# Attention, soft mixture of experts and MLP in one kernel: the code behind the attention re-ordered by hand, the spread of G moved from engine copies to DMAs

## The chip, the core and the metric

The kernel runs on one core of a Trainium2 chip. The metric is device time in microseconds for one execution. A core has TensorE (PE in the rows; PEld is its weight load), VectorE (DVE), ScalarE (ACT), GpSimd (POOL) and SyncE (SP), which here only issues DMAs, from one queue, in order. Each engine executes its own instructions strictly in the order of the program and waits for semaphores of the others.

## The reference

```
q, k: (4, 8, 576, 64), rotated by position; attn = softmax(q k^T / 8) v
x = attn as (2304, 512)
logits = x @ phi                            # (2304, 32): 8 experts x 4 slots
d = softmax of logits over the 2304 tokens
s = d.T @ x                                 # slot inputs, (32, 512)
slot_out[e] = relu(s[e] @ w1[e]) @ w2[e]    # w1 (8,512,1024), w2 (8,1024,512)
c = softmax of logits over the 32 slots
y = c @ slot_out                            # (2304, 512), of rank 32
h = y @ w_in; g = h * sigmoid(h)            # w_in (512, 2048)
out = g @ w_out                             # w_out (2048, 512)
```

`w_in` and `w_out` come as 64-bit floats and are narrowed on the chip.

## The kernel before

**Attention** (until about 285 us of the trace) runs over 16 pairs of heads in an order written out by hand. It is not touched, except that its last piece, pair 15, is followed by the soft maximum over tokens of the last batch, done in two halves (`half(0)`, `half(1)`, L530 to L621).

**The tail.** `half(h)` does: logits (L545, L548, tile `lgh`), their maximum (L558), the exponentials (L567, ACT), their transposition (`dps`, L584, L586), the weighted sums `sps` (L595 with 128 tokens each, L599 with the 64 left over), and for half 1 `slots()` (L605): the two halves' sums are scaled and added by DVE (L608), turned by four products with a stacked identity (`si_ps`, L614) and copied to `si`, the slot inputs (L615). `x_15(1)` (L448 to L452) turns the last 64 + 256 tokens of the attention's output, which the last quarter of half 1's logits needs. `lt3_ps` (L945) turns the logits for the combine weights; DVE copies it (L947, L948).

**Experts** (L964 to L1106). `layer1` (L974) and `layer2` (L995) hold 32 slots as four groups of 32 columns of the array, one expert each, and stream the weights `w_0` to `w_63`, 512 KB a load; `more()` issues four further loads after each group, into slots that become free. 27 loads are issued during the attention (`W_LOADS`), the rest when its memory is released. `hidden_t` and `slot_t` turn the results by full-array transposes (L985, L1008). `combine` (L1017) computes the combine weights c on ACT and DVE, `combine_split` splits them into a high and a low part, `combine_t(b)` (tile `cst`, L1054, five transposes each for four blocks b, then DVE casts, L1061) lays them out as `cs`. From here on a scheduler of the framework orders the instructions, not the source, except where `tc.manual_schedule()` stands.

**Opening of the last stage** (L1226 to L1245, order by hand). G = slot_out @ `w_in` (32 x 2048) is made in pieces: the first 128 columns (`g0_ps`, L1229), 384 more (`g_product(0)`, L1192, and `g_spread`, L1213), then three times 512 (`g_product(1..3)`). G must lie in four groups of 32 partitions (high, high, low, low part: the tile `gs`). For pieces 1 to 3 `g_copy` (L1201) copies each of four quarters of a piece into the four groups: 16 copies of 32 x 128 a piece, 12 by ACT (L1206) and 4 by DVE (L1208).

**Last stage.** Three blocks of 768 tokens times 16 steps k. `hidden(j, k)` makes h for 128 columns of G in two halves: `hps` (L1152, PE, two PSUM buffers in all), sigmoid (L1156, ACT), product (L1159, DVE), the high part `ghi` (L1162, ACT), the low part `glo` (L1165, DVE), which frees the PSUM buffer. A step then has 18 products of 512 columns into six sums `ops` (L1257 to L1259: high*high, high*low, low*high). In block 0 `w_out` is also prepared: load (L126), `narrow` (L136 on ACT, L139 and L142 on DVE), split into `wo_hi` (L1134, ACT) and `wo_lo` (L1135, POOL); four of sixteen pieces are narrowed during the attention (`W_OUT_EARLY`). The last quarter of `w_in` is narrowed there too (`conv_last`).

Two "warm" products (L1221, `dummy`) without use stand in the opening; the scheduler placed one of them between the products of layer 2.

## Time and profile before

| | |
|---|---|
| median of 3 runs | 569.34 us (567.28 to 569.64) |
| the profiled execution | 568.04 us, of which its span is 566.2 us |
| PE busy | 542.6 us, 96% of the span |
| DVE, ACT, POOL busy | 317.5, 309.0, 111.6 us |
| share of PE in the chain that ended last | 77% (ACT 10%, DVE 7%, DMA 2%) |
| DMA | 88.53 MB, 156 GB/s on average |

Times in the rows are us from the start of the span. The profiled execution lies 1.30 us under the median, and 1.84 us of it lie outside the span. A busy PE means that matmuls are in flight, not that they follow each other without gaps.

### The profile page before, as it was taken

The page shows a single profiled execution, that of the slowest core. Times are in us where ns is not written, and L with a number is a line of the kernel's source. Part 1 is how long each engine was busy: PE and PEld are TensorE (multiplying, and loading weights), DVE is VectorE, ACT ScalarE, POOL GpSimd, SP SyncE. Part 2 cuts the span into 40 slices and gives each one's busy share as a digit, 9 for nine tenths or more (in the row PEclk, how much of TensorE's full clock was granted, in tenths as well). Part 3 has the DMA queues.
Part 4 walks back from the last instruction along what each step waited for, and adds up shares of the span by engine and source line. Part 5 has one row for each costly group of instructions (what it writes and reads, how often), then busy time and mean ns, then how long its engine had stood idle before and what let it go on. Part 6 is the DMA issues. An engine that isn't in the chain of part 4 may idle for free.

```text
span 566.2 us, 15233 instructions
## 1 busy us (share of the span) xinstructions
PE 542.6 (96%) x6281; PEld 438.1 (77%) x6281; DVE 317.5 (56%) x844; ACT 309.0 (55%) x613; POOL 111.6 (20%) x103
## 2 busy tenths in 40 slices
PE   8989999999999999999989979898999999999997
PEld 5667888889888898888853347686888888888885
DVE  4667666676665566653142356897464444644442
ACT  3657767666776576664422247987454334543332
POOL 3475333412333333100001030141000000000000
PEclk9999999999999999999999999999999999999999
DMA  8325777655663585653789965440020000300002
GB/s 328 114 83 203 236 245 250 201 180 174 219 226 125 201 284 192 230 171 116 294 309 375 389 280 186 148 125 25 1 111 1 0 1 1 113 0 1 0 2 111
DMA packets 36417, 88.53 MB, mean 156 GB/s; under 512 B 9830, under 2 KB 11644, under 8 KB 34428
## 3 DMA queue, kind: packets, MB, share of 16 engines
q1 hardware_dynamic: 36348, 87.57, 44.2%
q8 instruction: 49, 0.80, 0.6%
q14 instruction: 20, 0.16, 0.1%
HBM read 78.20 MB, written 7.60 MB: 152 GB/s over the span
## 4 chain that ended last, share of the span: by engine, by line
PE 77%; ACT 10%; DVE 7%; issue 3%; DMA 2%; POOL 0%; SPq 0%; ACTq 0%; DVEq 0%
PE u L420 10%; PE ops L1259 10%; PE ops L1257 10%; PE ops L1258 10%; PE st L387 8%; PE psmx L316 3%; PE hps L1152 3%; PE st_r L400 3%; ACT e L391 3%; PE xps L448 2%; PE l L974 2%; ACT relu L324 2%; PE u L414 2%; PE psmx L332 2%; PE warm_up L841 2%
## 5 line engine op out<-in xcount | busy, mean ns | idle before, releaser
L1159 DVE TENSOR_TENSOR hps<-hps,g 128x384 f32<-128x384 f32 x96 | 49.8, 561 | 84.6 <-ACT g L1156 84.3
L1156 ACT ACTIVATE g<-hps 128x384 f32<-128x384 f32 x96 | 42.3, 490 | 82.3 <-PE hps L1152 82.0
L1257 PE MATMUL ops<-wo_hi,ghi 128*128 128x512 f32 x216 | 84.7, 392 | 0.0
L337 DVE CUSTOM_DVE_ANT_0 relu<-psmx,relu 128x288 f32<-128x288 f32 x142 | 59.3, 454 | 45.0 <-ACT e L391 38.0
L1258 PE MATMUL ops<-wo_lo,ghi 128*128 128x512 f32 x216 | 84.4, 391 | 0.0
L1259 PE MATMUL ops<-wo_hi,glo 128*128 128x512 f32 x216 | 84.3, 390 | 0.0
L391 ACT ACTIVATE e<-st 128x512 f32<-128x512 f32 (+1 forms) x128 | 76.4, 650 | 10.4 <-PE st L387 10.4
L420 PE MATMUL u<-v,e 128*64 128x65 f32 x2048 | 80.1, 224 | 0.3 <-ACT e L391 0.3
L420 PEld LDWEIGHTS u<-v,e 128*64 128x64 f32 x2048 | 70.8, 137 | 6.7 <-issue 2.4
L324 ACT ACTIVATE relu<-psmx 128x576 f32<-128x576 f32 x63 | 40.9, 651 | 53.6 <-PE psmx L316 41.9
L266 POOL TENSOR_TENSOR raw<-raw,tab 128x576 f32<-128x576 f32 x28 | 40.3, 1438 | 114.4 <-DMA raw<-in_qk_dram 94.8
L1165 DVE TENSOR_TENSOR glo<-hps,ghi 128x384 fp32r<-128x384 f32 x96 | 49.4, 552 | 4.9 <-ACT ghi L1162 1.8
L1162 ACT ACTIVATE ghi<-hps 128x384 fp32r<-128x384 f32 x96 | 45.6, 492 | 10.1 <-DVE hps L1159 10.1
L1259 PEld LDWEIGHTS ops<-wo_hi,glo 128*128 128x128 f32 x216 | 40.6, 188 | 8.5
L1258 PEld LDWEIGHTS ops<-wo_lo,ghi 128*128 128x128 f32 x216 | 40.6, 188 | 7.5 <-issue 0.4
L1257 PEld LDWEIGHTS ops<-wo_hi,ghi 128*128 128x128 f32 x216 | 40.5, 188 | 7.4 <-issue 0.2
L263 POOL TENSOR_TENSOR raw<-raw,tab 128x576 f32<-128x576 f32 x28 | 41.3, 1475 | 0.0
L387 PE MATMUL st<-hi 64*128 64x256 f32 (+1 forms) x256 | 39.2, 300 | 0.0
L387 PE MATMUL st<-mq,neg_a 64*128 64x256 f32 (+1 forms) x256 | 38.2, 292 | 0.0
L387 PE MATMUL st<-hi,lo 64*128 64x256 f32 (+1 forms) x256 | 38.1, 292 | 0.0
L387 PE MATMUL st<-lo,hi 64*128 64x256 f32 (+1 forms) x256 | 38.1, 292 | 0.0
L431 DVE TENSOR_SCALAR r<-u 128x4 f32<-128x4 f32 (+1 forms) x32 | 5.2, 163 | 51.1 <-PE u L422 30.9
(233 smaller groups left out, 1008.4 us busy)
## 6 DMA issues: line engine op xcount, KB each, us to landing
w<-in_w_dram SPq DMA_DIRECT2D x64, 512.0 KB
...
```

The lines of the kernel that those rows point to most:

```text
L324: act.activation(out=r, in_=pair[:, :, 0:HS], func=ACTF.Relu)
L337: dve.tensor_tensor_reduce(out=r[:, hd], in0=t[hd], in1=r[:, hd], scale=1.0, scalar=-3.0e38, op0=ALU.add, op1=ALU.max, accum_out=mxs[p % 2 ...
L387: pe.matmul(st[:, hd, 0:n], lhsT=a, rhs=b, start=i == 0, stop=i == 3, skip_group_check=True)
L391: act.activation(out=e[:, :, 0:n], in_=st[:, :, 0:n], func=ACTF.Exp, scale=0.125)
L420: pe.matmul(u[q:q + 64, 2 * i + hd], lhsT=e[:, hd, o:o + 64], rhs=x[:, hd], start=n == 0 and i + hd == 0, stop=n == 4, skip_group_check=True)
L1156: act.activation(out=g[i], in_=t[i], func=ACTF.Sigmoid)
L1159: dve.tensor_tensor(out=t[i], in0=t[i], in1=g[i], op=ALU.mult)
L1162: act.activation(out=ghi[:, i], in_=t[i], func=ACTF.Copy)
L1165: dve.tensor_tensor(out=glo[:, i], in0=t[i], in1=ghi[:, i].bitcast(F32), op=ALU.subtract)
L1257: pe.matmul(t, lhsT=a, rhs=wo_hi[k], start=k == 0, stop=False)
L1258: pe.matmul(t, lhsT=a, rhs=wo_lo[k], start=False, stop=False)
L1259: pe.matmul(t, lhsT=b, rhs=wo_hi[k], start=False, stop=k == 15)
```

## The change

Behind the attention it does the following.

- Tail: `x_15(1)` goes ahead of two thirds of half 1's logits; the sums of half 1 are put in four column groups instead of two (`s_mm`); what lies in `s_b` is turned by a scaled identity `ss`, half 1's sums are copied by ACT and turned with 64 rows each, both into the same sum, and one copy gives `si`; the logits' transposes stand between; their copies go from DVE to ACT, and the sum of exponentials (`total`) behind `si`.
- Experts: the order of the source holds (`manual_schedule`); `combine` comes after `hidden_t(1)`; the blocks 2 and 3 of `combine_t` stand behind the last product of layer 2, ahead of and behind the turn of its result; the dummy products are gone. One more weight load (`w_27`) is issued during the attention, into the memory of the rotary table, and the slots of those behind it are given in the order in which the attention releases memory.
- Opening: `w_out` piece 0 is among the early ones (0, 3, 6, 10 instead of 3, 6, 9, 12), so that the opening narrows piece 1 alone; `ghi`'s first half goes ahead of the copy of `g_product(0)`; three products stand ahead of `g_spread`. `wo_lo` 0 and 1 go from DVE to POOL.
- Last stage: the second half of `hidden` in block 0 comes one sum later than the first; the 48 copies of `g_copy` become 48 DMAs from SP, a quarter of a piece per step; the loads of `w_out` take the next of three buffers in turn.

**The tail on PE**, from the product that adds up half 0's logits (`xps15_1` is `x_15(1)`, `dps3` the transposes of half 0). Before:

```order
L555 MATMUL lgh0_4879<-last_logits_4878,cst_sb_73 128x256
L548 MATMUL lgh1_4915<-xt12_4349,phi_sb_75 32x320 x4
L548 MATMUL lgh1_4915<-xt13_4621,phi_sb_75 32x320 x4
L548 MATMUL lgh1_4915<-xt14_4831,phi_sb_75 32x320 x4
L584 MATMUL dps3_4931<-cst_sb_73,last_logits_4878 128x32 x2
L448 MATMUL xps15_1_4935<-cst_sb_73,x15_4803 64x128 x4
L450 MATMUL xps15_1_4935<-cst_sb_73,x15_4803 64x64 x2
L548 MATMUL lgh1_4915<-xt15_4844,phi_sb_75 32x320 x4
```

And now:

```order
L566 MATMUL lgh0_4881<-last_logits_4880,cst_sb_76 128x256
L559 MATMUL lgh1_4917<-xt12_4351,phi_sb_78 32x320 x4
L459 MATMUL xps15_1_4922<-cst_sb_76,x15_4805 64x128 x4
L461 MATMUL xps15_1_4922<-cst_sb_76,x15_4805 64x64 x2
L559 MATMUL lgh1_4917<-xt13_4623,phi_sb_78 32x320 x4
L559 MATMUL lgh1_4917<-xt14_4833,phi_sb_78 32x320 x4
L559 MATMUL lgh1_4917<-xt15_4846,phi_sb_78 32x320 x4
L596 MATMUL dps3_4945<-cst_sb_76,last_logits_4880 128x32 x2
```

The turn of the last tokens has moved ahead of two groups of logits, the transposes of half 0 behind all of them.

**The end of layer 2 on PE**, up to the first product of G (`l2_1` is layer 2's second sum, `otp1` the turn of its result). Before:

```order
L995 MATMUL l2_1_5291<-w_59_5137,ht1_5223 32x512 x2
L1054 MATMUL cst2_0_5355<-cst_sb_73,ch2_5318 128x128 x3
L1054 MATMUL cst2_1_5360<-cst_sb_73,ch2_5318 128x128
L1054 MATMUL cst2_1_5360<-cst_sb_73,ch2_5318 128x64
L1054 MATMUL cst3_0_5365<-cst_sb_73,ch3_5342 128x128 x3
L1054 MATMUL cst3_1_5370<-cst_sb_73,ch3_5342 128x128
L1054 MATMUL cst3_1_5370<-cst_sb_73,ch3_5342 128x64
L995 MATMUL l2_1_5291<-w_60_5147,ht1_5223 32x512 x2
L995 MATMUL l2_1_5291<-w_61_5149,ht1_5223 32x512 x2
L995 MATMUL l2_1_5291<-w_62_5151,ht1_5223 32x512 x2
L995 MATMUL l2_1_5291<-w_63_5153,ht1_5223 32x512 x2
L1008 MATMUL otp1_5386<-cst_sb_73,o1_5384 128x128 x4
```

And now:

```order
L1017 MATMUL l2_1_5294<-w_60_5152,ht1_5220 32x512 x2
L1017 MATMUL l2_1_5294<-w_61_5154,ht1_5220 32x512 x2
L1017 MATMUL l2_1_5294<-w_62_5156,ht1_5220 32x512 x2
L1017 MATMUL l2_1_5294<-w_63_5158,ht1_5220 32x512 x2
L1079 MATMUL cst2_0_5372<-cst_sb_76,ch2_5322 128x128 x3
L1079 MATMUL cst2_1_5377<-cst_sb_76,ch2_5322 128x128
L1079 MATMUL cst2_1_5377<-cst_sb_76,ch2_5322 128x64
L1033 MATMUL otp1_5382<-cst_sb_76,o1_5369 128x128 x4
L1079 MATMUL cst3_0_5388<-cst_sb_76,ch3_5346 128x128 x3
L1079 MATMUL cst3_1_5393<-cst_sb_76,ch3_5346 128x128
L1079 MATMUL cst3_1_5393<-cst_sb_76,ch3_5346 128x64
L1276 MATMUL g0_ps_5430<-w_in0_90,so_5090 32x128 x16
```

Layer 2 runs through, and block 2 of the combine weights stands where PE waits for ACT, block 3 where it waits for DVE.

**SP in block 0 now**, in place of the copies of L1206 and L1208 (`gs0` takes pieces 0 and 1 of G, `gh1` and `gl1` are piece 1's two parts):

```order
L187 DMA w_in_raw3_0_5282<-in_w_in_dram 128x2x1024
L133 DMA w_out_raw4_5512<-in_w_out_dram 128x1024
L133 DMA w_out_raw5_5514<-in_w_out_dram 128x1024
L133 DMA w_out_raw7_5533<-in_w_out_dram 128x1024
L1249 DMA gs0_5397<-gh1_5593 32x128 x2
L1249 DMA gs0_5397<-gl1_5594 32x128 x2
L133 DMA w_out_raw8_5630<-in_w_out_dram 128x1024
L1249 DMA gs0_5397<-gh1_5593 32x128 x2
L1249 DMA gs0_5397<-gl1_5594 32x128 x2
L133 DMA w_out_raw9_5679<-in_w_out_dram 128x1024
```

The DMAs of a quarter stand in SP's one queue, each time behind a load of `w_out` that waits until `narrow` has read its buffer.

The diff, cut:

```diff
--- before.py
+++ after.py
@@ -45,17 +45,21 @@
 W_IN_STEPS = (4, 4, 5)
 FETCH_AHEAD = 5
 BATCH = (22, 24, 24, 27, 28, 34)
-W_LOADS = (14, 18, 24, 27, 34, 37, 45, 54, 64, 66, 76, 86, 96, 102, 108, 114, 127, 129, 125, 135, 133, 123, 137, 145, 148, 134, 139)
+W_LOADS = (14, 18, 24, 27, 34, 37, 45, 54, 64, 66, 76, 86, 96, 102, 108, 114, 127, 129, 125, 135, 133, 123, 137, 145, 148, 134, 139, 138)
 SCALES = -19
-W_OUT_EARLY = (3, 6, 9, 12)
+W_OUT_EARLY = (0, 3, 6, 10)
 W_OUT_AT = (23, 43, 83, 113)
...
+WO_TAB = 11
+FREED = (0, 1, 2, 3, 4, 14, 17, 5, 6, 7, 8, 9, 10, 11, 12, 18, 19, 13, 15, 16)
 WO_SLOT = {12: 13, 13: 14, 14: 15, 15: 16}
 QO = (0, 256, 576)
 QN = (256, 320)
 
-G_STEPS = (5, 7, 16, 19, 28, 14, 23, 37, 46, 53, 58)
-ACT_QUADRANTS = (0, 1, 2)
+G_STEPS = (5, 25, 49)
+LOAD_STEP = 28
+SPREAD = (7, 27, 51)
+CONV_AT = (2, 5, 8, 9)
 
 
 @with_exitstack
...
                         act.activation(out=sc[:, 5:6], in_=mall[:, 1:2], func=ACTF.Exp, bias=nmb[:, 5:6])
-                        act.activation(out=s_b[0][64:128], in_=s_b[0][64:128], func=ACTF.Copy, scale=sc[64:128, 5:6])
+                        ps["ss"] = p_r.tile([128, 3, NSLOT], F32, tag="dh0", name="ss")[:, 0]
+                        dve.tensor_scalar(out=ps["ss"], in0=stack_i[:, 0:NSLOT], scalar1=sc[:, 5:6], scalar2=None, op0=ALU.mult)
 
...
-                    for j in range(4):
+                    js = (0, 2, 1, 3) if h else range(4)
+                    for j in js:
                         w = slice(128 * j, 128 * j + 128)
+                        g = 64 * h * (j // 2)
                         for c in range(2):
-                            pe.matmul(t[32 * c:32 * c + 32, w], lhsT=d[:, c], rhs=x_c(12 + j, 2 * h + c), start=j == 0, stop=h == 0, skip_group_check=True)
-                    for j in range(4 * h):
-                        for hd, r in enumerate(HEAD):
+                            pe.matmul(t[g + 32 * c:g + 32 * c + 32, w], lhsT=d[:, c], rhs=x_c(12 + j, 2 * h + c), start=j % (2 if h else 4) == 0, stop=h == 0, skip_group_check=True)
...
-                def slots():
-                    acc = s_b[0]
-                    for j in range(2):
-                        w = slice(256 * j, 256 * j + 256)
-                        dve.scalar_tensor_tensor(out=acc[0:64, w], in0=acc[0:64, w], scalar=sc[0:64, 5:6], in1=ps["s"][0:64, w], op0=ALU.mult, op1=ALU.add)
-                    t2 = ps_mx.tile([128, 2, 512], F32, tag="mx", name="si_ps")
-                    for j in range(2):
-                        t = t2[:, j]
-                        for k in range(2):
-                            c0 = 256 * j + 128 * k
-                            pe.matmul(t[:, NSLOT * k:NSLOT * k + NSLOT], lhsT=acc[:, c0:c0 + 128], rhs=stack_i[:, 0:NSLOT], start=True, stop=True)
-                        dve.tensor_copy(out=si[:, 2 * j:2 * j + 2], in_=t[:, 0:64].rearrange("p (k s) -> p k s", k=2))
+                def slots(between):
+                    o = hb[1][:, 0:DM]
+                    t = ps_st.tile([128, 2, 512], F32, tag="st", name="slots")[:, :, 0:2 * NSLOT].rearrange("p b (k s) -> p b k s", k=2)
+                    for r, c in ((slice(0, 64), slice(0, 256)), (slice(64, 128), slice(256, 512))):
+                        act.activation(out=o[r, c], in_=ps["s"][r, c], func=ACTF.Copy)
+                    for k in range(4):
+                        pe.matmul(t[:, k // 2, k % 2], lhsT=s_b[0][:, 128 * k:128 * k + 128], rhs=ps["ss"], start=k % 2 == 0, stop=False, skip_group_check=True)
+                    between()
+                    for k in range(4):
+                        r = HEAD[k // 2]
+                        pe.matmul(t[:, k // 2, k % 2], lhsT=o[r, 128 * k:128 * k + 128], rhs=stack_i[r, 0:NSLOT], start=False, stop=True, skip_group_check=True)
+                    dve.tensor_copy(out=si.rearrange("p (b k) s -> p b k s", b=2), in_=t)
+
...
+                for i, (o, n) in enumerate(CHUNKS[3]):
+                    pe.transpose(t[0:n, 0, NSLOT * i:NSLOT * i + NSLOT], hb[2][0:32, o:o + n], ident[0:32, 0:32])
+
             h1[6]()
-            t = ps_st.tile([128, 2, 512], F32, tag="st", name="lt3_ps")[:, 0]
-            for i, (o, n) in enumerate(CHUNKS[3]):
-                pe.transpose(t[0:n, NSLOT * i:NSLOT * i + NSLOT], hb[2][0:32, o:o + n], ident[0:32, 0:32])
-            h1[7]()
-            dve.tensor_copy(out=lt[:, 15:19], in_=t[:, 0:4 * NSLOT].rearrange("p (c s) -> p c s", c=4))
-            dve.tensor_copy(out=lt[0:64, 19], in_=t[0:64, 4 * NSLOT:5 * NSLOT])
+            h1[7](lt3)
+            act.activation(out=lt[:, 15:19], in_=t[:, 0, 0:4 * NSLOT].rearrange("p (c s) -> p c s", c=4), func=ACTF.Copy)
+            act.activation(out=lt[0:64, 19], in_=t[0:64, 0, 4 * NSLOT:5 * NSLOT], func=ACTF.Copy)
+            h1[9]()
 
         def pool2(name, bufs, space=None, st=ctx, **kw):
             kw.update({"reuse_waits": "tile"}, **({"space": space} if space else {}))
...
-        for i in range(NWA + 4, NW):
-            slot_w(i)
-        for i in range(NWA + 4, NW):
+        for i in range(NW - NWA - 5):
+            slot_w(NWA + 5 + FREED.index(i))
+        for i in range(NWA + 5, NW):
...
-        def slot_t(g):
+        def slot_t(g, between=None):
             o = mid.tile([128, DM], F32, tag=f"s_b{g}", name=f"o{g}")
-            act.activation(out=o, in_=op[g], func=ACTF.Copy)
+            for c in (slice(0, 256), slice(256, 512)):
+                act.activation(out=o[:, c], in_=op[g][:, c], func=ACTF.Copy)
+            if between:
+                between()
...
+        order = ExitStack()
+        order.enter_context(tc.manual_schedule())
-        combine()
-        layer2(0, (lambda: hidden_t(1),))
+
+        def h2():
+            hidden_t(1)
+            combine()
+
+        layer2(0, (h2,))
+        load_in(0)
         load_wo(0)
-        load_in(0)
+        load_in(1)
         load_wo(1)
-        load_in(1)
-        load_wo(2)
...
-            combine_t(2)
-            combine_t(3)
-            t, h = (wa.tile([128, 2, 512], F32, tag=f"w{i}", name=n) for i, n in ((3, "wf_first"), (4, "hw_first")))
-            for k in range(2):
-                first.append((t[:, k], narrow(raw_w.pop(k), t[:, k], None, None, hw=h[:, k])))
+            t, h = (wa.tile([128, 512], F32, tag=f"w{i}", name=n) for i, n in ((3, "wf_first"), (4, "hw_first")))
+            first.append((t, narrow(raw_w.pop(1), t, None, None, hw=h)))
...
-        slot_t(1)
-
-        for f in first[0][1]:
-            f()
+        slot_t(1, lambda: combine_t(2))
+        combine_t(3)
+
         gs2 = [spare(10, "gs0")]
+        order.close()
...
-            between()
-            for f, i in ((f3, 0), (f4, 0), (f3, 1), (f4, 1)):
+            copy = between(0)
+            f3(0)
+            copy()
+            for f, i in ((f4, 0), (f3, 1), (f4, 1)):
                 f(i)
+        elif j == 0:
+            f0(0)
+            f1(0)
+            f2(0)
+
+            def rest():
+                for f in (f0, f1, f2):
+                    f(1)
+                if k + 1 in LATE:
+                    narrow_wo(k + 1)
+                    load_wo(LATE.index(k + 1) + 3)
+                elif k in CONV_AT:
+                    conv_last(CONV_AT.index(k))
+                for f in (f3, f4):
+                    for i in range(2):
+                        f(i)
+                if k > 1:
+                    split_hl(k, wf_early[k])
+                if k + 1 in LATE and k in CONV_AT:
+                    conv_last(CONV_AT.index(k))
+
+            later.append(rest)
...
+        c0 = 512 * (n % 2) + 128 * r
         for q in range(4):
-            c0 = 512 * (n % 2) + 128 * r
-            o, i = gs2[n // 2][32 * q:32 * q + 32, c0:c0 + 128], gfull[n][q // 2][32 * r:32 * r + 32].bitcast(F32)
-            if q in ACT_QUADRANTS:
-                act.activation(out=o, in_=i, func=ACTF.Copy)
-            else:
-                dve.tensor_copy(out=o, in_=i)
+            sp.dma_start(out=gs2[n // 2][32 * q:32 * q + 32, c0:c0 + 128].bitcast(F32), in_=gfull[n][q // 2][32 * r:32 * r + 32].bitcast(F32))
...
-        split_hl(1, wf1, dve)
-        gs2.append(spare(4, "gs1"))
...
+    order.enter_context(tc.manual_schedule())
+    wf1, n1 = first[0]
+    split_hl(0, wf_early[0])
...
+    hidden(*seq[0], between=g_product)
+    products(0, 0, 0, *gt[0, 0])
+    g_spread()
+    for i in (1, 2):
+        products(0, 0, i, *gt[0, 0])
...
+    split_hl(1, wf1)
+    gs2.append(spare(4, "gs1"))
+    order.close()
+    for i in (2, 3):
+        load_wo(i)
...
+    later.pop()()
...
+    for n in range(1, 4):
+        put(G_STEPS[n - 1], lambda n=n: g_product(n))
         for r in range(4):
-            g_copy(n, r)
-
-    extra = {}
-    for x, f in zip(G_STEPS, (lambda: g_product(1), lambda: copies(1), lambda: g_product(2), lambda: copies(2), lambda: load_last(1),
-                              lambda: conv_last(0), lambda: conv_last(1), lambda: conv_last(2), lambda: conv_last(3), lambda: g_product(3), lambda: copies(3))):
-        extra.setdefault(divmod(x, 6), []).append(f)
-    ops = {}
+            put(SPREAD[n - 1] + NI * r, lambda n=n, r=r: g_copy(n, r))
+    put(LOAD_STEP, lambda: load_last(1))
...
+            if (j, k, i) not in ((0, 0, 0), (0, 0, 1), (0, 0, 2)):
+                products(j, k, i, ghi, glo)
...
+            elif i == 3 and later:
+                later.pop()()
```

## Rows read from the trace of the kernel before

**Rows 1.** The page, part 2: TensorE's granted clock in 40 slices, tenths.

```profile
PEclk9999999999999999999999999999999999999999
```

**Rows 2.** Timeline of the tail: start, us, engine, line, what, [idle before <-releaser].

```profile
284.90 1.82 PE L548 MATMUL lgh<-xt,phi_sb 128*32 128x320 f32 x24
...
286.89 0.66 PE L448 MATMUL xps<-cst_sb,x 128*64 128x128 f32 x8
...
288.20 0.75 PE L548 MATMUL lgh<-xt,phi_sb 128*32 128x320 f32 x8 [0.54 <-ACT xt L452]
...
293.16 0.86 DVE L608 SCALAR_TENSOR_TENSOR s_b<-s_b,sc,sps 64x256 f32<-64x256 f32 x2 [1.15 <-PE sps L599]
...
295.20 1.07 PE L974 MATMUL l<-w,si 128*32 128x512 f32 x8
...
296.86 0.64 PE L974 MATMUL l<-w,si 128*32 128x512 f32 x4 [0.59 <-DVE lt L948]
```

**Rows 3.** Timeline of layer 2.

```profile
315.87 0.70 PE L1221 MATMUL warm<-cst_sb 128*128 128x256 f32 x2
...
316.49 5.41 PE L995 MATMUL l<-w,ht 128*32 128x512 f32 x48
...
327.81 0.42 PEld L1054 LDWEIGHTS cst<-cst_sb,ch 128*128 128x128 f32 x4 [0.84 <-issue]
327.81 0.86 PE L1054 MATMUL cst<-cst_sb,ch 128*128 128x128 f32 x5
...
329.86 1.94 PE L995 MATMUL l<-w,ht 128*32 128x512 f32 x16
```

**Rows 4.** Timeline of the opening.

```profile
333.55 1.08 PE L1229 MATMUL g_ps<-w_in,so 128*32 128x128 f32 x32 [0.32 <-DVE so L1011]
...
334.72 1.64 DVE L142 SCALAR_TENSOR_TENSOR wf_first<-w_out_raw,wf_first 128x512 uint32<-128x512 uint32 x1
336.39 0.29 DVE L1032 TENSOR_TENSOR gs<-g_ps,gs 64x128 fp32r<-64x128 f32 x1
...
336.74 0.61 PE L1152 MATMUL hps<-cs,gs 128*128 128x384 f32 x2 [1.05 <-DVE gs L1032]
337.22 0.87 ACT L1156 ACTIVATE g<-hps 128x384 f32<-128x384 f32 x2 [2.25 <-PE hps L1152]
...
337.74 1.03 DVE L1159 TENSOR_TENSOR hps<-hps,g 128x384 f32<-128x384 f32 x2 [1.06 <-ACT g L1156]
...
338.62 0.89 ACT L1162 ACTIVATE ghi<-hps 128x384 fp32r<-128x384 f32 x2
...
338.89 1.10 PE L1213 MATMUL g_all<-gf,w_in_n 128*128 128x96 f32 x8 [0.74 <-ACT gf L1195]
...
339.77 0.48 PE L1257 MATMUL ops<-wo_hi,ghi 128*128 128x512 f32 x1
```

**Rows 5.** The chain that ended last, in the last stage: start, us, what.

```profile
404.99 0.35 PE hps L1152 x2
...
409.44 0.34 PE hps L1152 x2
```

**Rows 6.** Waits, 339.7 to 400 us: us in total, times, longest.

```profile
PEld hps L1152 <- DVE glo L1165: 4.5, 8, 1.6
...
PEld g_ps L1192 <- DVE glo L1165: 2.6, 3, 1.9
```

**Rows 7.** Groups, 339.7 to 400 us: busy us, mean ns of one, idle before.

```profile
L1135 POOL TENSOR_TENSOR wo_lo<-wf,wo_hi 128x512 fp32r<-128x512 f32 x7 | 10.1, 1438 | 34.7 <-ACT wo_hi L1134 34.7
...
L1206 ACT ACTIVATE gs<-gh 32x128 fp32r<-32x128 f32 x24 | 7.4, 309 | 0.4
```

**Rows 8.** The DMAs of the tile out_dram: ns min/median/max of the issue, first and last start.

```profile
L1272 SPq DMA_DIRECT2D out_dram<-os x18: 332/332/423, 417.6 to 563.1; - x18
```

**Rows 9.** Stretches of 2 us: busy of PE, PEld, DVE, ACT, POOL, PEclk, DMA share, GB/s.

```profile
322.00:324.00 2.00, 2.00 (x17) 1.18 (x20) 1.31 (x4) 0.56 (x2) 0.00 (x0) 1.00 1.06 391
334.00:336.00 2.00, 1.69 (x28) 1.03 (x20) 1.79 (x2) 0.94 (x3) 2.00 (x3) 1.00 0.55 221
```

More of the change, by code (lines that the diff above doesn't have):

```diff
@@ L146, in attn_softmoe_mlp_kernel, with load_wo @@
     raw_w, wf_early = {}, {}
-    def load_wo(k):
-        if k in W_OUT_EARLY:
-            return
-        raw_w[k] = load_64(w_out[128 * k:128 * k + 128], wa, f"w{k % 3}", f"w_out_raw{k}")
+    LATE = [k for k in range(16) if k not in W_OUT_EARLY]
+    def load_wo(i):
+        if i < len(LATE):
+            k = LATE[i]
+            raw_w[k] = load_64(w_out[128 * k:128 * k + 128], wa, f"w{i % 3}", f"w_out_raw{k}")
     w_next, gfull, raw_in, sel = {}, {}, {}, []
@@ L620, in slots @@
                     dve.reciprocal(out=den, in_=den)
-                return logits, logits2, soft, expo, keep, d_t, s_mm, slots, merge
+                return logits, logits2, soft, expo, keep, d_t, s_mm, slots, merge, total
             CHUNKS = [[(128 * c, min(128, S - 128 * c)) for c in range(5)]] * 4
@@ L696, in attn_softmoe_mlp_kernel @@
                 at(g + 6, lambda k=k: cv["o", k][1](), lambda k=k: cv["o", k][2]())
-            for i in range(NWA + 4):
+            for i in range(NWA + 5):
                 at(W_LOADS[i], lambda i=i: load_w(i))
@@ L1049, in combine_t @@
                 o0 = CHUNKS[b][sel[0]][0]
[L1050 removed]
+                t = (ps_h if b > 1 else ps_t).tile([128, 512], F32, tag="h" if b > 1 else "t", name=f"cst{b}_{part}")
                 n = 0
@@ L1239, in attn_softmoe_mlp_kernel, with products @@
-    hidden(*seq[1])
-    def copies(n):
-        for r in range(4):
-            g_copy(n, r)
-    extra = {}
-    for x, f in zip(G_STEPS, (lambda: g_product(1), lambda: copies(1), lambda: g_product(2), lambda: copies(2), lambda: load_last(1),
-                              lambda: conv_last(0), lambda: conv_last(1), lambda: conv_last(2), lambda: conv_last(3), lambda: g_product(3), lambda: copies(3))):
-        extra.setdefault(divmod(x, 6), []).append(f)
-    ops = {}
+    ops = {}
+    def products(j, k, i, ghi, glo):
+        if k == 0:
+            ops[j, i] = ps_o.tile([128, DM], F32, tag="o", name=f"ops{j}_{i}")
+        t = ops[j, i]
+        a, b = ghi[:, 128 * i:128 * i + 128], glo[:, 128 * i:128 * i + 128]
+        pe.matmul(t, lhsT=a, rhs=wo_hi[k], start=k == 0, stop=False)
+        pe.matmul(t, lhsT=a, rhs=wo_lo[k], start=False, stop=False)
+        pe.matmul(t, lhsT=b, rhs=wo_hi[k], start=False, stop=k == 15)
```

85 lines of the change are left out of this document (38 added, 47 removed).

## The prediction

> **What bounds the kernel now.** I read the page's clock row first: TensorE was granted 1.00 of its clock, the upper level of 2.4 GHz, in all 40 slices, the tail included, where it idles for most of some microseconds [rows 1]. PE is busy for 96% of the span, so the sum below counts where PE waits or does something that the change takes off it. The chain of waits gives the price of a step of the last stage once it runs freely: two successive `hps` of that stage start at 404.99 and 409.44, so a step takes 4.45 us [rows 5]. The change leaves the 18 products of a step alone, and from about 405 us on there is nothing to gain. What is left lies between 285 and 405 us: the tail, two interruptions of layer 2, the dependent opening, and the first part of block 0. The timeline gave the first three, the list of waits the fourth.
>
> **A, the tail: 1.7 us gained.** *Last tokens earlier.* Before, PE does 24 logits products (1.82 us from 284.90), two transposes, then the turn of the last tokens (0.66), and waits 0.54 us for ACT's copy `xt`; the last quarter of the logits starts at 288.20 [rows 2]. With the turn ahead, only PE's own work is left: 284.90 + 1.82 + 0.66 = 287.4, and 0.8 us would be gained. But ACT's copies stand in line with the exponentials of half 0; I take 0.5 (0 to 0.8). *Slots.* From DVE's sums at 293.16 to layer 1 at 295.20 is 2.04 us: two scalings of 0.43, four products, two copies [rows 2]. Now: two ACT copies side by side with four products that need no copy, four more products, one DVE copy, about 1.6 by the same rows; 0.4 gained. As the products switch from 128 to 64 rows in between, which these rows don't price, the bounds are 0.4 lost and 0.8 gained. *Sums in four column groups.* Half 1's sums have twice as many groups side by side; the four-group products of layer 1 are the nearest row (8 of 512 columns in 1.07 us, 0.13 each [rows 2]); with 32 short products to save on I take 0.2 (0 to 0.6). *Copies of the transposed logits.* Layer 1's second part waits 0.59 us for DVE's copy `lt` [rows 2]; on ACT, that is free there, it doesn't: 0.6 (0.5 to 0.8). Sum 1.7, bounds 0.1 and 3.0.
>
> The nearest row on switching is the start of the full-array transposes behind layer 2's 32-column products: the weight load stood idle 0.84 us for nothing that the trace names [rows 3]. That row has a semaphore's wait in it, so it is no clean price, and the sum goes by 1.7. The Trainium skill, page "TensorEngine Tiling (Array Packing)", section "Key Properties", says that TensorE drains when the tiling mode is changed; the new tail does that twice more, and by that rule and half of that idle time for the two together A would be worth 1.3 and the total 559.4. No run so far shows which.
>
> **B, experts: 2.67 us.** Two `warm` products without use lie between layer 2's products: 316.49 - 315.87 = 0.62 us. Blocks 2 and 3 of the combine weights hold PE from 327.81 to the next product at 329.86, 2.05 us [rows 3]. Afterwards block 2 stands where PE waits for ACT behind the last product, block 3 where it waits for DVE; what they cost there is counted under C. That `hidden_t(1)` and `combine` change places I count as nothing (0.4 either way), because ACT and DVE have the whole of layer 2 for it. The lower bound is 0.6: PE would wait at the end of layer 2 for weights anyway. I don't expect that. The queue moves 391 GB/s at 322 to 324 us and has run low by 334 to 336 (221 GB/s) [rows 9]. Behind `w_63` seven loads were issued by then, of 512 KB five times, 768 and 1024 KB, 4.35 MB, or 11.2 us at that rate, before the queue ran dry at about 335; `w_63` had thus landed near 324, the extra early load makes it 1.35 us earlier, and the faster PE wants it at 326 to 327.
>
> **C, opening: 1.3 us.** Let T be the end of layer 2, before 329.86 + 1.94 = 331.80 [rows 3]. The first product `ops` starts at 339.77, T + 7.97. In it, DVE's half of `gs` ends at 336.39 + 0.29, T + 4.88, only because the 1.64 us `wf_first` stands ahead of it [rows 4]. That operation is gone. New: 1.75 from T to `g_ps` as before, 0.6 for block 3 (0.86 on PE, part of it beside DVE's copy of `so`), 1.14 for `g_ps`, 0.57 for the split on ACT and DVE (DVE's row has 0.29): T + 4.06, a gain of 0.8. From `hps` at 336.74 to `ops` took 3.03 us; by the same durations the sigmoid starts 0.48 later, the first product on DVE at 1.00, takes 0.52, and half a `ghi` takes 0.45: 2.05 with an issue gap, a gain of 1.0 as `ops` no longer stands behind `g_spread`. `g_spread` itself (`g_all`, 1.1 us of PE [rows 4]) moves into the products; about half of it falls in a wait of the first steps: 0.5 back. Bounds: 0.5 lost (all of `g_spread` and block 3 are on the path, DVE is late for another reason) and 2.0 gained.
>
> **D, block 0: 4.6 us.** From 339.77 to 404.99 are 65.2 us. They hold 225 products and 13 pairs of `hps`, that is 12.5 steps of 4.45 and a pair, 55.8 us. The excess is 9.4; three times `g_ps` (1.08 each, [rows 4]) is work that stays, 3.2; so PE stalled for 6.2. The list of waits agrees: `hps` waits for `glo` 4.5 us in 8 stalls, `g_ps` 2.6 in 3 [rows 6], since `glo` frees the PSUM buffers and DVE comes to it late. DVE and ACT are late because `g_copy` puts 48 copies ahead of that work: ACT has 36 of them at 309 ns, 11 us (24 are in the row of `gh`, those of `gl` and DVE's are of the same size) [rows 7], and because both wait in order for `w_out` to arrive and be narrowed. The 48 DMAs take SP's time, not theirs. I leave 1.6 us: `wo_lo` 1 takes 1.44 us now that it is on POOL [rows 7], a third of it, 0.5, at step 1; two buffer waits of 0.3 around the pieces; 0.5 for a late first quarter. Bounds 0 (another operation of the same two engines is late instead) and 6.2.
>
> The quarters' price isn't in the trace of before. A DMA's issue costs SP 0.33 us, and the 256 KB of the last output land within 3.1 us of an issue at 563.1 (span end 566.2) [rows 8]; a quarter has 64 KB in four DMAs, so 3.1 us is its upper bound on an idle queue. Piece 1's `gl1` is ready about 5 us into the stage, its first quarter is wanted about 4 us later: a margin near 1 us, and 0.6 to 3 us at the later ones by the order of the steps.
>
> **Sum.** 1.7 + 2.67 + 1.3 + 4.6 = 10.3 us. The profiled execution of 568.04 gives 557.7. It lies 1.30 under the median of 569.34, so the prediction is **559.0 us**. The best bounds together (3.0, 2.7, 2.0, 6.2) give 555.4; the worst together no gain.
>
> **Rivals.**
> 1. *Block 0 keeps its stalls* (D = 0): 559.0 + 4.6 = 563.6. For it: the waits end at `glo`, and DVE and ACT still have the narrowing and the splits of twelve pieces in order. Against: in that stretch the copies alone are 11 us of ACT. Chance 0.14.
> 2. *Expert weights set T*, A and B are lost in a wait for `w_60` to `w_63`: 559.0 + 4.4 = 563.4. For it: the queue is full until 324 [rows 9], and the slots' order is new. Against: 2 to 3 us of margin. Chance 0.05.
> 3. *Slower: the quarters come late.* SP is one queue in order, and each quarter stands behind a load of `w_out` that waits until `narrow` has read its buffer. If `narrow` is late, the quarter is late, `hps` of the next steps waits, and `narrow` of the next step with it. There are 12 quarters; the gain of 10.3 is gone from 0.86 us per quarter on. At 1.5 us each, 18 us are lost: 577. For it: half the landing bound would do. Against: three buffers let a load run three pieces ahead. Chance 0.08.
> 4. *The clock falls.* With the `warm` products gone, PE has idle gaps in tail and opening. Granted 1.2 GHz, a step takes 4.45 us more; one step so gives 563.5. Against: the clock was 1.00 in all slices [rows 1], and the tail has no such products and gaps just as long. Chance 0.04. The Trainium skill, page "TensorE: Matmul & The Clock Gate", section "Part 1: The HAM clock gate", says that the throttled state is the default and activity releases it; no slice here shows the lower level.
> 5. *It doesn't do what it says*: the scheduler had filled the gaps as well, and what is taken from them comes back as other waits, 567 to 570. Chance 0.04.
>
> **How the numbers follow.** The forecast has the remaining 0.65. Its own range is 555.4, by all best bounds, to 562. The range of 554.5 to 565.5 takes in rivals 1, 2 and 4 and leaves out the slow one and no change. 0.5% is 2.85 us, about what a measurement of this kernel can tell from no change; faster means under 566.5. Faster: the forecast, rivals 1, 2, 4, less 0.05 for two of them at once: 0.83. Same 0.07, slower 0.10.
>
> **What would show it.** A: `xps15_1` before two groups of logits, and no wait for `lt` ahead of layer 1's second part. B: no `warm` and no `cst` between the products of layer 2, whose end lies near 327.4. C: the first `ops` near 333.6. D: the `hps`-for-`glo` and `g_ps`-for-`glo` waits together under 2 us instead of 7.1, no copies of `gs` from `gh` on ACT or DVE, step and clock as before. Wrong it would be if `hps` waited for DMAs of `gs`, if PE's weight loads of layer 2 waited for `w`, or if the sum of `glo` waits stayed above 4 us.

## The result and the profile after

Changed kernel: 562.17 us median of 4 runs (560.96 to 563.53); kernel before, beside it: 569.21 us (567.28 to 569.64). The ratio is 0.9893, 95% interval 0.9864 to 0.9921: faster by 7.0 us where 10.3 were forecast. The profiled execution took 562.48 us (span 560.7).

From the start of one product to the start of another on PE, worked out from the timelines; `again` is a second profile of the same changed kernel (e11_again below). The bounds are the product that adds up half 0's logits, the first of layer 1, the first and the last of layer 2, the first `hps`, the first `ops`, the 217th and the last `ops`.

| stretch, us | before | after | again |
|---|---|---|---|
| start to the tail | 284.27 | 283.70 | 282.92 |
| tail | 10.93 | 10.24 | 10.02 |
| layer 1 | 15.72 | 17.78 | 14.92 |
| layer 2 | 20.29 | 17.15 | 17.15 |
| end of layer 2 to `hps` | 5.53 | 4.75 | 4.75 |
| `hps` to `ops` | 3.03 | 2.14 | 2.14 |
| 12 steps | 63.01 | 61.12 | 61.12 |
| the rest | 159.1 | 159.2 | 159.2 |

Layer 2, the opening and the steps agree to 0.01 us between the two profiles of the changed kernel. That the tail starts 0.57 us earlier than before (1.36 in `again`) is no part of the change: the 0.57 us lie in the first products of the attention (`warm_up`, 9.41 us instead of 9.98), which the change leaves alone. Layer 1 differs by 2.86 us between the two, and in the first of them it is *longer* than before. The page's clock row of the changed kernel shows why, where [rows 1] had none:

```profile
PEclk9999999999999999999998999999999999999999
```

Stretches around it (columns as in [rows 9]; the clock is the number ahead of the last two), of the changed kernel:

```profile
290.00:292.00 2.00, 1.66 (x39) 1.37 (x39) 0.91 (x2) 0.50 (x2) 0.00 (x0) 1.00 1.04 394
292.00:294.00 2.00, 1.61 (x21) 1.40 (x24) 0.36 (x3) 0.61 (x3) 0.00 (x0) 0.73 1.02 390
294.00:296.00 2.00, 2.00 (x12) 0.54 (x16) 0.69 (x4) 0.00 (x0) 0.00 (x0) 0.50 1.04 384
...
298.00:300.00 2.00, 2.00 (x16) 0.51 (x12) 0.00 (x0) 0.00 (x0) 0.00 (x0) 0.56 0.91 305
300.00:302.00 2.00, 2.00 (x27) 0.49 (x19) 0.00 (x0) 0.00 (x0) 0.00 (x0) 1.00 1.00 349
```

TensorE runs at its lower level, 1.2 GHz, from about 293 to 300 us, while layer 1 streams. Timeline of layer 1's first 96 products in the changed kernel:

```profile
293.95 13.37 PE L996 MATMUL l<-w,si 128*32 128x512 f32 x96 [0.39 <-DVE si L630]
```

and in its second profile, at full clock:

```profile
292.93 10.51 PE L996 MATMUL l<-w,si 128*32 128x512 f32 x96 [0.40 <-DVE si L630]
```

They are the same products in the same order; only the clock differs. The order of the tail is as forecast: the turn of the last tokens (L459) stands ahead of 24 logits products, and neither those nor layer 1 waits for ACT's `xt` or for `lt` any more [rows 2].

```profile
285.01 0.66 PE L459 MATMUL xps<-cst_sb,x 128*64 128x128 f32 x8
...
285.71 1.82 PE L559 MATMUL lgh<-xt,phi_sb 128*32 128x320 f32 x24
```

Layer 2 and the opening of the changed kernel, PE's timeline:

```profile
314.61 7.14 PE L1017 MATMUL l<-w,ht 128*32 128x512 f32 x64
...
325.79 3.68 PE L1017 MATMUL l<-w,ht 128*32 128x512 f32 x32
329.40 0.86 PE L1079 MATMUL cst<-cst_sb,ch 128*128 128x128 f32 x5
330.19 0.66 PE L1033 MATMUL otp<-cst_sb,o 128*128 128x128 f32 x4
330.68 0.80 PE L1079 MATMUL cst<-cst_sb,ch 128*128 128x128 f32 x5
331.82 1.08 PE L1276 MATMUL g_ps<-w_in,so 128*32 128x128 f32 x32 [0.34 <-DVE cs L1086]
333.63 0.62 PE L1173 MATMUL hps<-cs,gs 128*128 128x384 f32 x2 [0.72 <-DVE gs L1057]
...
335.77 0.50 PE L1266 MATMUL ops<-wo_hi,ghi 128*128 128x512 f32 x1 [0.73 <-ACT ghi L1183]
...
336.70 1.02 PE L1254 MATMUL g_all<-gf,w_in_n 128*128 128x96 f32 x8
```

No `warm` and no `cst` stand between the products of layer 2 [rows 3]; `g_all` now stands behind the first product instead of ahead of it [rows 4]. PE's waits in block 0 of the changed kernel (us, times, longest; against [rows 6]):

```profile
PEld hps L1173 <- DVE glo L1186: 1.6, 4, 0.6
PEld g_ps L1237 <- DVE glo L1186: 1.1, 3, 0.4
...
PEld ops L1267 <- POOL wo_lo L1161: 0.8, 1, 0.8
```

The waits for `glo` fell from 7.1 to 2.7 us (forecast: under 2), and none for a DMA of `gs` stands in the list. A new one, for `wo_lo` 1 on POOL, came in.

### The profile page after: what moved, and what is told of

It is laid out like the page before. It is cut to its first block, busy times and chain, and to the rows that moved or that the text cites. A ratio compares the mean times of both kernels' runs of the same rounds, so it can differ in the third digit from the quotient of the medians.

```text
span 560.7 us, 15277 instructions
## 1 busy us (share of the span) xinstructions
PE 542.5 (97%) x6283; PEld 437.4 (78%) x6283; DVE 312.7 (56%) x826; ACT 298.8 (53%) x582; POOL 112.5 (20%) x105
## 4 chain that ended last, share of the span: by engine, by line
PE 81%; ACT 7%; DVE 5%; issue 3%; DMA 2%; SPq 1%; ACTq 0%; DVEq 0%
PE ops L1266 11%; PE ops L1268 11%; PE ops L1267 11%; PE u L431 10%; PE st L398 7%; PE psmx L327 3%; PE l L996 3%; PE hps L1173 3%; ACT e L402 3%; PE st_r L411 3%; PE l L1017 3%; PE xps L459 2%; ACT relu L335 2%; PE u L425 2%; PE psmx L343 2%
## 5 line engine op out<-in xcount | busy, mean ns | idle before, releaser
L1266 PE MATMUL ops<-wo_hi,ghi 128*128 128x512 f32 x198 | 77.8, 393 | 0.7 <-ACT ghi L1183 0.7
L1267 PE MATMUL ops<-wo_lo,ghi 128*128 128x512 f32 x198 | 77.4, 391 | 0.3 <-POOL wo_lo L1161 0.3
L1268 PE MATMUL ops<-wo_hi,glo 128*128 128x512 f32 x198 | 77.6, 392 | 0.0
L1183 ACT ACTIVATE ghi<-hps 128x384 fp32r<-128x384 f32 x96 | 46.2, 491 | 10.4 <-DVE hps L1180 10.3
L1268 PEld LDWEIGHTS ops<-wo_hi,glo 128*128 128x128 f32 x198 | 37.2, 188 | 8.1 <-DVE glo L1186 0.3
L1266 PEld LDWEIGHTS ops<-wo_hi,ghi 128*128 128x128 f32 x198 | 37.2, 188 | 7.9 <-ACT ghi L1183 0.9
L1267 PEld LDWEIGHTS ops<-wo_lo,ghi 128*128 128x128 f32 x198 | 37.2, 188 | 7.1 <-POOL wo_lo L1161 0.8
L1266 PE MATMUL ops<-wo_hl,ghi 128*128 128x512 f32 x90 | 35.2, 391 | 0.0
```

Of the source, the lines that this page charges most:

```text
L1183: act.activation(out=ghi[:, i], in_=t[i], func=ACTF.Copy)
L1266: pe.matmul(t, lhsT=a, rhs=wo_hi[k], start=k == 0, stop=False)
L1267: pe.matmul(t, lhsT=a, rhs=wo_lo[k], start=False, stop=False)
L1268: pe.matmul(t, lhsT=b, rhs=wo_hi[k], start=False, stop=k == 15)
```

## The experiments

Theory after the result: the parts work about as forecast, and what is missing went to the clock in the tail and to new costs in block 0. Rivals: that the clock was chance, that single parts gave nothing, and that the order of block 0, not the DMAs, took the stalls away. Whole times scatter by about 1 us (the stretch ahead of the tail, whose products are the same in all versions, took 282.9 to 284.8 us in the profiles, and 287.1 in e7_cst), so a part is judged by its stretch. The mean clock of each run tells what the clock took at most.

**e11_again: is the loss of clock an accident?** No edit.

> The changed kernel itself once more, beside the next three on the same chip. Theory: the loss of clock in the tail is no accident of the four runs seen so far; most runs show a mean clock of 0.992 to 0.997, and the median is 561.5 to 562.8 us, while the mean clock of the kernel before lies at 0.997. Rival: the four runs were unlucky; half of the runs or more show 0.999 to 1.000 and the median is 559 to 560 us.

561.64 us (558.61 to 563.24), ratio 0.9887 (0.9857 to 0.9917). Mean clocks 1.000, 0.992, 0.997, 0.992, 0.997, 0.996: the theory held. The mean clock of the changed kernel is 0.9950 over all its runs (10, one at 0.999 or more), that of the kernel before 0.9971 over those beside the experiments (51, 17 such). One minus the clock, times the span, bounds the time lost: 2.8 us against 1.6. It is a bound because the clock is also low at the end of the span, behind PE's last product, where it costs nothing; in the first profile of the changed kernel:

```profile
559.17:560.70 1.53, 0.00 (x0) 0.00 (x0) 0.00 (x0) 0.00 (x0) 0.00 (x0) 0.50 0.00 0
```

The profile before, at 1.00 throughout, was thus not typical of its kernel either. Beside these six runs stand eleven of the kernel before with a median of 567.65 us; the gain by the ratio is 6.4 us.

**e1_warm: fill the gaps of the tail.** Four products without use, `idle` into a free bank of `lgh1`:

```diff
+h1[10](1, 128)   # idle(n, w), behind each wait of PE in the tail
```

> The changed kernel with four products of 128 columns without use added in the tail, one in each place where PE waits there (behind the transposes of half 0, behind the sums of half 0, behind the transposes of half 1, ahead of layer 1). Theory: TensorE's clock falls to 1.2 GHz at the end of the changed tail because PE does too little there; with the gaps filled it stays at 1.00, layer 1's first 96 products take 10.7 us instead of 13.4, and the time is 562.2 - 2.6 = 559.6 us. Rival: gaps of this size stood in the tail before, too, and the clock did not fall there, so it is not the idle time that matters; the clock still falls and the time is 562 to 563 us.

560.09 us (559.29 to 563.95), ratio 0.9871 (0.9844 to 0.9898); four of six runs at 1.000, of 559.3 to 560.2 us. In its profile layer 1's 96 products took 10.51 us, but now the clock fell in the opening:

```profile
332.00:334.00 2.00, 1.26 (x35) 0.81 (x34) 1.15 (x3) 1.52 (x5) 1.91 (x2) 1.00 0.17 61
334.00:336.00 2.00, 2.00 (x8) 1.61 (x8) 0.96 (x2) 0.37 (x1) 0.00 (x0) 0.54 0.02 4
336.00:338.00 2.00, 2.00 (x9) 1.82 (x9) 0.42 (x1) 0.94 (x3) 0.00 (x0) 0.61 0.00 0
```

The 12 steps took 62.29 us there instead of 61.12, and the four products made the tail 0.8 us longer (10.82 against 10.02 in e11_again). The clock holds more often; that the kernel is faster for it is not shown, as the intervals of its ratio and of the changed kernel's overlap.

**e2_slots: the sums and slots of before.** `s_mm` in two groups, DVE scales and adds, `si_ps` with two copies.

> The changed kernel with the sums of half 1 in two column groups and the slots as before (DVE scales and adds, four products with the stacked identity, two copies). Theory: the clock falls because of what the new slots put ahead of layer 1 (sixteen short products, half of them on 64 rows, and the wait for one copy); with the old ones it stays at 1.00, layer 1 starts about 0.6 us later and takes 2.6 less: about 560.2 us. Rival: the clock falls wherever the tail's short products end; then 562.2 + 0.6 = 562.8 us.

560.63 us (559.70 to 561.46), ratio 0.9867 (0.9844 to 0.9890). Layer 1 at full clock (14.92 us), three of four runs at 0.999 or more, one with the fall in the opening. The tail took 10.42 us against 10.02 of the changed kernel at full clock, so the new slots and sums together are worth 0.4 us. The two do not share it as forecast. The sums of half 1 and what follows them, before:

```profile
291.42 1.07 PE L595 MATMUL sps<-x,dh 128*32 128x128 f32 x16 [0.36 <-DVE dh L588]
...
292.99 0.46 PE L945 MATMUL lt_ps<-cst_sb,last_logits 32*128 32x32 f32 x5
```

and in the changed kernel:

```profile
290.35 0.65 PE L609 MATMUL sps<-x,dh 128*32 128x128 f32 x16 [0.36 <-DVE dh L600]
...
291.28 1.08 PE L625 MATMUL slots<-ss,s_b 128*128 128x32 f32 x8
...
292.29 0.46 PE L964 MATMUL lt_ps<-cst_sb,last_logits 32*128 32x32 f32 x5
```

The sums fell from 1.57 to 0.93 us (1.57 again in e2_slots). From there to layer 1 it took 2.21 us before and in e2_slots, but 2.45 with the new slots at full clock (e11_again): these lose 0.24 us.

The mean clock of e2_slots leaves at most 0.7 us of loss, against 2.8 for the changed kernel, which is more than the 0.4; the whole times overlap. PE idles no less in this tail than in the changed one (busy 5.70 us of 286 to 292.9, against 5.93, up to where the clock of the latter fell), and e11_again, with the same 5.93 us at the same place of its tail, kept its clock: idle time alone is not what decides.

**e3_x15: the turn of the last tokens back.**

```diff
-h1[0]((0,)); x_15(1); h1[0]((1, 2))
+h1[0]((0, 1, 2))
 h0[3]()
-h1[0]((3,)); h0[5]()
+h0[5](); x_15(1); h1[0]((3,))
```

> The changed kernel with the turn of the last tokens back behind two thirds of half 1's logits. Theory: that step gave 0.5 us (0 to 0.8) and has nothing to do with the clock, which still falls: about 562.7 us. Rival: the order of the logits decides how much PE does in the tail; then the clock stays at 1.00 and the time is about 560.1 us.

561.34 us (560.77 to 562.19), ratio 0.9877 (0.9851 to 0.9902). From the product that adds up half 0's logits to the sums of half 1, ahead of the clock's fall, it takes 7.15 us again, as before, instead of 6.64: 0.5 us for this step. The clock fell still (0.992, 0.992, 0.995, 1.000).

**e4_copies: the quarters of G by engines again**, in the new order.

```diff
-sp.dma_start(out=gs2[...].bitcast(F32), in_=gfull[...].bitcast(F32))
+(act.activation if q < 3 else dve.tensor_copy)   # the copies of before
```

> The changed kernel with the quarters of G copied by the engines again (three of four by ACT, one by DVE), at the steps where the DMAs now stand. Theory: the 48 copies were what made ACT and DVE late in block 0, and the stalls of PE there come back: 2 to 4 us slower, 564 to 566 us, with PE's waits of hps and g_ps for glo back at 4 us or more. Rival: the stalls went because hidden and the narrowing of w_out were put in another order; then within 0.7 us of 562.2.

568.65 us (567.16 to 569.79), ratio 1.0005 (0.9990 to 1.0019): all of the gain is gone. 12 steps later than its first product, at 336.52, it stands at 404.48:

```profile
336.52 0.50 PE L1270 MATMUL ops<-wo_hi,ghi 128*128 128x512 f32 x1 [0.73 <-ACT ghi L1183]
...
404.48 0.39 PE L1270 MATMUL ops<-wo_hl,ghi 128*128 128x512 f32 x1
```

67.96 us against 61.12; `hps` waits 6.1 us for `glo`. The theory held, with a larger price than I gave it, 6.8 us.

**e6_dma: the DMAs alone**, in the kernel before.

> The kernel before with one part of the change alone: its 48 copies of G's quarters are DMAs from SP, at the places where the copies stood (sixteen at once for each piece). Theory: the copies make ACT and DVE late, and the stalls of block 0 go with them: 4 to 6 us faster than before, 563 to 565 us. Rival: it takes the new order of block 0 as well, since sixteen DMAs stand behind a load of w_out that waits and the piece comes too late: 568 to 572 us.

565.25 us (563.32 to 565.88), ratio 0.9955 (0.9937 to 0.9973). Its steps:

```profile
340.87 0.48 PE L1254 MATMUL ops<-wo_hi,ghi 128*128 128x512 f32 x1
...
400.05 0.39 PE L1254 MATMUL ops<-wo_hl,ghi 128*128 128x512 f32 x1
```

59.18 us instead of 63.01, a gain of 3.8. The whole gained 2.5 us by the ratio, less than the 4 to 6 expected; in the profile the clock fell in layer 1 (17.25 us instead of 15.72) behind a tail that is that of before. So the DMAs alone take more out of the 12 steps than the change as a whole did (1.89). The difference lies in the first two steps, 5.68 and 6.99 us in the changed kernel against 4.59 and 6.18 here. `g_all` is about 0.9 of it, which the kernel before has ahead of its first product (the products around it start at 336.36 and 337.51, 1.15 us apart instead of 0.23); step 1 is the one that `wo_lo` 1 lengthens (e10_wo1).

**e7_cst: blocks 2 and 3 back between the products of layer 2.**

```diff
 def t3():
+    combine_t(2); combine_t(3)
-slot_t(1, lambda: combine_t(2)); combine_t(3)
+slot_t(1)
```

> The changed kernel with blocks 2 and 3 of the combine weights back between the products of layer 2, one after the other ahead of its last quarter. Theory: there they cost 2.05 us and behind layer 2 they cost 0.3 to 0.9 us, so it is 1.2 to 1.8 us slower than the changed kernel, at the same clock. Rival: behind layer 2 they stand on the path from the sum to G and cost as much as between the products: within 0.4 us of the changed kernel.

Ratio 0.9947 (0.9921 to 0.9972), nine runs of 560.5 to 567.0 us (mean 564.8); a tenth took 2898 us, for a reason that is not known, and is not counted. The blocks side by side:

```profile
329.41 1.65 PE L1079 MATMUL cst<-cst_sb,ch 128*128 128x128 f32 x10
330.98 1.94 PE L1017 MATMUL l<-w,ht 128*32 128x512 f32 x16
333.46 0.71 PE L1033 MATMUL otp<-cst_sb,o 128*128 128x128 f32 x4 [0.54 <-ACT o L1028]
```

Layer 2 is 1.72 us longer, the way from there to `hps` 0.78 shorter: behind layer 2 the blocks cost 0.8 instead of 1.7, 0.9 gained, less than expected. 12 steps took 62.01 us, 0.9 more. What made those late was not followed up. In this profile, the one with the latest tail, the clock fell twice: in the attention (0.50 at 222 to 224 us) and in layer 1 (0.58 at 296 to 300).

**e5_warm2: e1_warm, and products without use in the opening.**

```diff
+idle(ps_h, "h", 1, 256)    # behind g0_ps
+idle(ps_o, "o", 1, 256)    # behind g_product(0)
```

> The kernel of e1_warm with two more products without use, of 256 columns each, in the opening: behind the first piece of G and behind the second, where PE waits for DVE and ACT. Theory: the loss of clock moves to the next stretch in which PE waits (in e1_warm's trace the opening and the first step ran at 0.54 to 0.61); with both stretches filled the clock is 1.00 in every run and the time is that of e1_warm's runs at 1.000, 559.3 to 560.2 us, with no run above 561. Rival: what is added in the opening stands on the path of the first products and costs what it saves: 560.5 to 561.5 us.

560.59 us (559.07 to 563.84), ratio 0.9873 (0.9845 to 0.9901). The theory fell: the profiled execution lost its clock in the filled tail, at 293 to 300 us. The profiles of e8_whole and e12_late, with the same products added, lost it there too. Mean clocks 0.994 to 1.000, on average 0.998 as in e1_warm.

**e8_whole: both halves of `hidden` together**, on e5_warm2.

```diff
 if i == 2 and n + 2 < len(seq):
     hidden(*seq[n + 2])
-elif i == 3 and later:
-    later.pop()()
+    if later: later.pop()()
```

> The kernel of e5_warm2 with both halves of hidden in block 0 issued one after the other again, behind the third sum. Theory: the split costs PE 0.04 us a step (4.49 instead of 4.45 in the steps without stalls) and hides nothing now that the copies are gone: 0.5 us faster than e5_warm2. Rival: DVE cannot free both buffers of hps in time, and PE's waits of hps for glo come back: 1 to 4 us slower than e5_warm2.

559.24 us (558.85 to 562.98), ratio 0.9866 (0.9830 to 0.9902). Steps without stalls take 4.45 us instead of 4.49, the 12 steps 60.88 instead of 61.10 in e5_warm2, and the waits for `glo` stay at 1.6 us. The split costs 0.2 us and, with the copies gone, brings nothing.

**e10_wo1: `wo_lo` 1 on DVE**, on e8_whole.

```diff
-split_hl(1, wf1)
+split_hl(1, wf1, dve)
```

> The kernel of e8_whole with wo_lo 1 on DVE instead of POOL. Theory: step 1 loses 1.5 us by wo_lo 1 on POOL: the product waits for it, and DVE's narrowing that starts while POOL works lasts until POOL has ended (1.42 us instead of 0.43), so that glo and the next hps come late. On DVE step 1 takes 5.6 to 6.2 us instead of 7.0. Rival: DVE is the one that is late; 0.7 us more on it keeps step 1 at 6.7 us or more.

561.99 us (560.60 to 565.89), ratio 0.9907 (0.9876 to 0.9939). Step 1 fell from 7.04 to 6.09 us, as the theory said; but step 4 rose from 5.88 to 7.09, and 12 steps took 61.81 us, 0.9 more. The later pieces, still on POOL, now met DVE's narrowing at other places: in step 4 one took 1.65 us (L149 at 359.30, behind POOL's from 359.11).

**e12_late: the low parts of all late pieces on DVE**, on e10_wo1.

```diff
-split_hl(k, wf_early[k])
+split_hl(k, wf_early[k], dve if k in LATE else pool)
```

> The kernel of e10_wo1 with the low parts of all late pieces of w_out on DVE, none on POOL. Theory (DVE is held up by POOL): the narrowing takes 0.43 us each time, and steps 3 and 4 (5.4 and 5.9 us) become shorter by 0.3 us or more each. Rival (DVE is full): 0.7 us more on it in each of eleven steps delays glo, and PE's waits of hps for glo grow by 1 to 4 us in all.

559.41 us (557.57 to 561.88), ratio 0.9856 (0.9829 to 0.9883). The 12 steps:

```profile
337.62 0.50 PE L1275 MATMUL ops<-wo_hi,ghi 128*128 128x512 f32 x1
...
396.67 0.39 PE L1275 MATMUL ops<-wo_hl,ghi 128*128 128x512 f32 x1
```

59.05 us, 1.8 less than e8_whole and 2.1 less than the changed kernel, although DVE has twelve operations of 0.68 us more (`wo_lo` 1 and the eleven of this step), and 2.8 less than e10_wo1. No wait of `hps` for `glo` is left, so the rival fell; steps 3 and 4 take 4.80 and 5.67 us, of which only step 3 gained the 0.3 expected. The reason stands in the timeline of the changed kernel:

```profile
349.27 0.43 DVE L146 TENSOR_SCALAR wf<-hwo 128x512 uint32<-128x512 uint32 x1
...
352.11 1.29 POOL L1161 TENSOR_TENSOR wo_lo<-wf,wo_hi 128x512 fp32r<-128x512 f32 x1 [6.26 <-ACT wo_hi L1160]
352.21 1.47 DVE L146 TENSOR_SCALAR wf<-hwo 128x512 uint32<-128x512 uint32 x1
```

The same DVE operation takes 0.43 us alone; started 0.1 us behind POOL's, it ends 0.28 us after it. One that starts ahead of POOL's is not held: L149 at 355.01 took its 0.69 us, and POOL's from 355.15 took 1.71 instead of 1.29. At step 1 this is what made `glo`, and with it `hps`, late (1.42 us from 341.00, beside POOL's from 340.85). The groups of e12_late, where POOL has nothing to do behind 337.6 us,

```profile
L149 DVE SCALAR_TENSOR_TENSOR wf<-w_out_raw,wf 128x512 uint32<-128x512 uint32 x11 | 7.5, 681 | 0.0
L146 DVE TENSOR_SCALAR wf<-hwo 128x512 uint32<-128x512 uint32 x11 | 4.6, 418 | 0.0
```

against those of the changed kernel, both from 335 to 392 us (busy us, mean ns, idle before):

```profile
L149 DVE SCALAR_TENSOR_TENSOR wf<-w_out_raw,wf 128x512 uint32<-128x512 uint32 x11 | 8.6, 783 | 0.2
L146 DVE TENSOR_SCALAR wf<-hwo 128x512 uint32<-128x512 uint32 x11 | 7.0, 640 | 0.4
```

The kernel before has the same lengthening (339.7 to 400 us; its L139 is L146 here):

```profile
L139 DVE TENSOR_SCALAR wf<-hwo 128x512 uint32<-128x512 uint32 x10 | 6.1, 606 | 1.4 <-ACT hwo L136 1.4
```

**e9_slots: old slots, filled opening, whole halves, `wo_lo` 1 on DVE.**

> The changed kernel with the sums and slots of before (as in e2_slots), the two products without use in the opening (as in e5_warm2, none in the tail), hidden of block 0 whole (as in e8_whole), and wo_lo 1 on DVE. Theory: the tail with DVE's slots loses 0.2 us and rarely the clock, the opening keeps it, whole halves give 0.5 and wo_lo 1 on DVE 0.5 to 1: 558.3 to 559.3 us. Rival: in the opening, too, the clock falls in half of the runs: 559.5 to 561 us.

561.30 us (560.45 to 561.84), ratio 0.9887 (0.9869 to 0.9905). The clock held best of all (0.998 to 1.000), but `wo_lo` 1 on DVE cost as in e10_wo1 (12 steps 61.41 us); a miss.

e12_late beats the kernel before clearly. Its median is 2.2 us under e11_again's beside it; the intervals overlap, and what is sure is the 2.1 us in the steps.

## Why the prediction was right, and where not

The direction and the range held. Without the clock, the parts make 8.3 us instead of 10.3; most of the difference is D. The runs agree: those of the kernel before at a mean clock of 0.999 or more have a median of 566.82 us (17 runs), the one such run of the changed kernel took 558.61. The 1.3 us from there to the 7.0 measured fit the clock, by which the changed kernel loses more (at most 2.8 us against 1.6).

- **A, the tail.** At full clock (e11_again) tail and layer 1 take 24.94 us instead of 26.65: 1.7 us, as forecast, in part by luck. The turn of the last tokens gave 0.5 (0.5 forecast) and layer 1 without its wait 0.8 (0.6). The sums in four groups gave 0.64 (0.2), and the new slots lost 0.24 where 0.4 of gain stood: two errors that cancel. The sum of the slots left out that the logits' transposes, beside DVE's scaling before, now stand on PE between the slots' products (0.4 us there; not tested by itself). Whether a change of tiling mode cost anything, as the Trainium skill's rule (page "TensorEngine Tiling (Array Packing)", section "Key Properties") would have it, cannot be told from the 1.7 against 1.3: the two errors are larger than the 0.4 between them.
- **B, experts.** 3.14 us instead of 2.67; both named interruptions are gone, and no long wait for weights came (one of 0.3 us). Rival 2 did not occur. The rest is that each interruption was priced from its own start to that of the next product: the stretches that held them are 0.77 and 2.19 us shorter, not 0.62 and 2.05, and the one with `hidden_t` is 0.18 shorter. (The seven loads behind `w_63` are 4.46 MB, 11.4 us at that rate; nothing hangs on the difference.)
- **C, opening.** 0.78 up to `hps` (0.8 forecast) and 0.89 to `ops` (1.0 forecast). The term that failed is "about half of it falls in a wait": `g_all` takes about 0.9 between the products of the first step, where no wait stands. What `ops` won by not standing behind it is paid back, and 0.8 remains of 1.3. That no later wait would have taken some of it up was not tested.
- **D, block 0.** 1.89 us, or 2.8 without `g_all`, instead of 4.6: the term that was off most. Its mechanism was right: copies by engines make ACT and DVE late (e4_copies, e6_dma), the DMAs are not late (rival 3 did not occur). Steps 2 to 11 gained 3.8 us (48.45 instead of 52.25), as the 12 steps of e6_dma did; steps 0 and 1 took 1.9 back (12.67 instead of 10.76). "I leave 1.6 us" was wrong: by the same sum 61.12 - 12 * 4.45 - 3 * 1.08 - 0.9 = 3.6 of 6.4 us of stalls are left, so rival 1 came true in part. I priced `wo_lo` 1 by its own length alone, not by what it does to DVE's narrowing (step 1 is 0.8 us longer), left out the split of `hidden` (0.2), and did not see that the low parts on POOL held up the narrowing in the kernel before too, which the DMAs do not change. With these on DVE and without the split, 59.05 us by the same sum leave 1.5, the size that I forecast, but the change does not do that.
- **Rival 4, the clock,** had 0.04 and came true: the first profile lost 2.86 us in layer 1, the runs at most 2.8 on average. I had read the clock row of one profile as the kernel's habit (its digits say 0.9 or more in each slice; the mean of 1.000 says that nothing fell). The kernel before loses at most 1.6 us on average, so it was half there already; the place was named (gaps in the tail), the size (4.45 in one step) was not met. The Trainium skill's rule (page "TensorE: Matmul & The Clock Gate", section "Part 1: The HAM clock gate") that activity holds the clock agrees with the direction: unfilled tails with the new slots had 3 of 33 runs at 0.999 or more, the same with fillers 17 of 28.

What stays open: what lets the clock fall. e2_slots and e9_slots (7 of 10 such runs, with PE in e2_slots no busier) point to the slots and sums, but these were not taken apart further; e6_dma shows a fall behind the tail of before, e11_again none behind the new one, and the added products did not keep it away in three of five profiles (e5_warm2, e8_whole, e12_late).
